# The last four output tiles of a fused attention and gated-MLP kernel: PSUM taken out by ScalarE, a bf16 gate, additions over whole rows

## The chip, the core and the metric

The kernel runs on one core of a Trainium2 chip. The core has five engines with queues of their own: TensorE (PE in the profile; its weight loads are PEld), VectorE (DVE), ScalarE (ACT), GpSimd (POOL) and SyncE (SP), which here only issues DMAs. The metric is the device time of one launch in microseconds, as the median of several runs. The profile comes from one profiled execution with a time of its own.

## The reference

Two blocks read the same normalised input and are multiplied together:

```python
xn = _layernorm(x, axis=-1)                      # x: 1 x 2048 x 640
qkv = xn @ wqkv                                  # 32 heads of 20
p = softmax(q k^T * 20**-0.5)
s = (p v) @ wo                                   # 2048 x 640
h = sigmoid(xn @ w_gate) * (xn @ w_up)           # 2048 x 1728
g = silu(h @ w_down)                             # 2048 x 640
return x + s * g
```

## The kernel before

Attention is worked off in 32 blocks: a block is one group of four heads and one chunk of 512 query rows. TensorE makes scores into PSUM. ScalarE takes most of them through Exp, and VectorE computes the others with integer operations on bf16 bits (L1030, L1033, L1036). TensorE multiplies the results with v into the bank `oacc`. Between these pieces a planner written in Python places the MLP of the four chunks, the projections of the next groups and the output projection of finished rows. It steps through a modelled time, decides what each engine does next from modelled durations, and so writes out the fixed order of the instructions on each engine. Only this order counts on the chip; between engines semaphores hold what depends on what.

**The gate.** `mk_down` (L720) multiplies the hidden layer with `w_down`. ScalarE takes tanh of it, and VectorE makes from tanh and PSUM four times the gate (L737 for the last chunk, L741 for the others). The gate of the first three chunks goes to DRAM and comes back later. That of the last chunk stays in SBUF as fp32, in two buffers of the tag `wgu`, which no longer hold weights by then: `gq_last(t4)` (L714) gives the 640 columns of row tile `t4`.

**The end stage.** The last block needs a path of its own, since nothing is left that could hide its latency. The last chunk has 512 rows, in four tiles of 128 rows (`t4` 0 to 3) with 640 columns. Before the end TensorE has done the output projection of these tiles for all but the last of five slices of the contraction (`early`, L1056), as its time allowed. It lies in PSUM in two parts: columns 0 to 511 of tile `t4` in the bank `mains[t4]`, and columns 512 to 639 of tiles 0, 1 together in `rest[0]`, of tiles 2, 3 in `rest[1]`. The list `chain` (L1135) then orders what is left. Each entry names an engine, a modelled duration, the function and the entries that it comes after. An engine runs its entries in the order of the list:

- `e_on`, `e_tr`, `e_scale`, `e_back`, `e_o`: in two halves of 256 rows the attention's result is taken out of `oacc`, transposed, divided by the sums, transposed back and copied into `oU`; half 0 by VectorE, half 1 by ScalarE where the two are named.
- `e_late(i)`: TensorE adds the last slice for the tiles of half `i`: first the two banks of 512 columns (L1093), then the two pieces of 128 columns (L1100). Of half 1, all narrow matmuls are done here.
- `t_main(t4)` (L1106): VectorE multiplies the bank with 0.25 and the gate into SBUF as bf16 (L1107); for tiles 0 and 1 GpSimd adds the 512 columns to the rows of x (L1110).
- `t_done(i)` (L1128): `t_rest` does the same for the 2 x 128 columns left over (VectorE L1113; the addition L1117 by GpSimd for half 0, by VectorE for half 1). For half 1 `t_last` (L1121) adds the 512 columns on VectorE. `t_out` (L1123) issues the store of each tile of 160 KB: even tiles from SyncE's queue, odd ones from ScalarE's.

The rows of x (`tail`) are loaded into SBUF long before (L1049) and hold the sum in the end. The products lie in `hfl`, the buffer of the hidden layer (`hT` in the profile), which is not needed any more; x and the sum lie in `xnT`.

So VectorE's order in the end stage is: products of banks 0 and 1, narrow product of half 0, products of banks 2 and 3, narrow product of half 1, narrow addition of half 1, additions of tiles 2 and 3. GpSimd's is: additions of tiles 0 and 1 and the narrow addition of half 0.

Of the kernel before, what the change touches and what calls it, by code (L numbers as in the profile page):

```python
# [52 lines left out]
def kernel(  # L53
# [22 lines left out]
    HD = D // 2  # L76
# [3 lines left out]
    def act_imm(o, i, func, scale):  # L80
        zero = mybir.ImmediateValue(dtype=FP32, value=0.0)
        sc = mybir.ImmediateValue(dtype=FP32, value=scale)
        return nc.scalar.add_instruction(mybir.InstActivation(  # L83
            func=func, name=nc.get_next_instruction_name(), engine=ENG.Activation,
            ins=[nc.scalar.lower_ap(i), zero, sc, zero], outs=[nc.scalar.lower_ap(o)]))
# [119 lines left out]
    with tc.tile_pool(name="ln", bufs=2) as lp, \  # L205
# [149 lines left out]
        for c in range(NQC):  # L355
            ks = range(4 * c, 4 * c + 4)
            st = [Step(s_stats, (k,), {"ACT": 1.83} if k in ACT_STATS else {"DVE": 1.03},
                       (table,) if k in ACT_STATS else (), X_AT[k], late=L_ST * c) for k in ks]
# [22 lines left out]
        t = 0.0  # L381
# [37 lines left out]
    def misc_ps():  # L419
        return bank[got_bank[0]]  # L420
# [48 lines left out]
    def mark(*e):  # L469
        return lambda t: ev_at.__setitem__(e, t)  # L470

    def cols(out, lhsT, rhs, start, stop):
        for j in range(0, P, 32):
            nc.tensor.matmul(out[j:j + 32, :], lhsT=lhsT[:, j:j + 32], rhs=rhs, start=start, stop=stop,  # L474
                             tile_position=(0, j), skip_group_check=True)
# [235 lines left out]

    gq_l = []

    def gq_last(t4):  # L714
        if len(gq_l) == t4 // 2:
            w = w2.tile([P, 2, KD, 2 * P], BF16, tag="wgu", bufs=2, name="gql")
            gq_l.append(w.rearrange("p i k f -> p (i k f)").bitcast(FP32))
        return gq_l[t4 // 2][:, t4 % 2 * D:(t4 % 2 + 1) * D]

    def mk_down(c, t4, h, at):  # L720
        st = {}
        tt = 4 * c + t4

        def alloc():
            st["ps"] = misc_ps()

        def mm(kf):
            cols(st["ps"][:, 0:HD], hT[:, kf, t4 * P:(t4 + 1) * P], wd[:, kf, h * HD:(h + 1) * HD],
                 kf == 0, kf == NFT - 1)

        def th():
            st["td"] = w2.tile([P, HD], BF16, tag="td", bufs=2, name="td")
            act_imm(st["td"], st["ps"][:, 0:HD], ACT.Tanh, 0.25)

        def ev():
            if c == NQC - 1:
                return nc.vector.scalar_tensor_tensor(out=gq_last(t4)[:, h * HD:(h + 1) * HD], in0=st["td"], scalar=1.0,  # L737
                                                      in1=st["ps"][:, 0:HD], op0=ALU.add, op1=ALU.mult)
            flush("o")
            gqs = w2.tile([P, HD], FP32, tag="gqs", bufs=3, name="gqs")  # L740
            ins = nc.vector.scalar_tensor_tensor(out=gqs, in0=st["td"], scalar=1.0, in1=st["ps"][:, 0:HD],  # L741
                                                 op0=ALU.add, op1=ALU.mult)
            nc.sync.dma_start(out=gq_dram[tt * P:(tt + 1) * P, h * HD:(h + 1) * HD], in_=gqs)
            return ins
        return Item([("PE", alloc, [(0.14, lambda kf=kf: mm(kf)) for kf in range(NFT)]),
                     ("ACT", 0.32, th), ("DVE", 0.40, ev, "free", mark("d", c, t4, h))], at, pre=[("h", c, kf) for kf in range(NFT)])
# [215 lines left out]
    def flush(*kinds):  # L962
        for x in [x for x in pool_q if x[1] in kinds]:
            pool_q.remove(x)
            x[2]()
# [74 lines left out]
    hfl = hT.rearrange("p k s -> p (k s)")  # L1040
    EX = D - 512
    xl = xfl[:, (NQC - 1) * KD * QC:(NQC - 1) * KD * QC + 4 * D]
    tail = []
# [8 lines left out]
    mains = [bank[0], bank[1], scA[1][:, 0, :], scA[1][:, 1, :]]  # L1052
# [38 lines left out]
    def e_late(i):  # L1091
        for t4 in (2 * i, 2 * i + 1):
            late_mm(mains[t4], t4, slice(0, 512))  # L1093
        if i:
            rest[1] = psum.tile([P, QC], FP32, name="rest1", tag="scA0")
            for kd in range(KD - 1):
                for t4 in (2, 3):
                    early(ex(t4), t4, slice(512, D), kd, t4 == 2)
        for t4 in (2 * i, 2 * i + 1):
            late_mm(ex(t4), t4, slice(512, D))  # L1100

    tmps = [hfl[:, t4 * 512:(t4 + 1) * 512] for t4 in range(4)]
    tmp = hfl[:, 4 * 512:4 * 512 + 4 * EX].rearrange("p (t e) -> p t e", e=EX)
    xg = xl.rearrange("p (t u) -> p t u", u=D)

    def t_main(t4):  # L1106
        nc.vector.scalar_tensor_tensor(out=tmps[t4], in0=mains[t4], scalar=0.25, in1=gq_last(t4)[:, 0:512],  # L1107
                                       op0=ALU.mult, op1=ALU.mult)
        if t4 < 2:
            nc.gpsimd.tensor_tensor(out=tail[t4][:, 0:512], in0=tmps[t4], in1=tail[t4][:, 0:512], op=ALU.add)  # L1110

    def t_rest(i):
        nc.vector.scalar_tensor_tensor(out=tmp[:, 2 * i:2 * i + 2, :],  # L1113
                                       in0=rest[i][:, 0:2 * EX].rearrange("p (t e) -> p t e", e=EX),
                                       scalar=0.25, in1=gq_l[i].rearrange("p (t u) -> p t u", u=D)[:, :, 512:D],
                                       op0=ALU.mult, op1=ALU.mult)
        (nc.vector if i else nc.gpsimd).tensor_tensor(out=xg[:, 2 * i:2 * i + 2, 512:D], in0=tmp[:, 2 * i:2 * i + 2, :],  # L1117
                                                      in1=xg[:, 2 * i:2 * i + 2, 512:D], op=ALU.add)

    def t_last(t4):  # L1120
        nc.vector.tensor_tensor(out=tail[t4][:, 0:512], in0=tmps[t4], in1=tail[t4][:, 0:512], op=ALU.add)  # L1121

    def t_out(t4):  # L1123
        r = slice(4 * (NQC - 1) * P + t4 * P, 4 * (NQC - 1) * P + (t4 + 1) * P)
        eng = nc.sync if t4 % 2 == 0 else nc.scalar
        eng.dma_start(out=out2[r, :], in_=tail[t4])

    def t_done(i):  # L1128
        t_rest(i)
        for t4 in (2 * i, 2 * i + 1):  # L1130
            if i:
                t_last(t4)
            t_out(t4)

    chain = [("DVE", 0.34, lambda: e_on(0), ()), ("ACT", 0.34, lambda: e_on(1), (0,)),  # L1135
# [2 lines left out]
             ("PE", 0.20, lambda: e_back(0), (4,)), ("PE", 0.20, lambda: e_back(1), (5,)),  # L1138
             ("DVE", 0.27, lambda: e_o(0), (6,)), ("ACT", 0.34, lambda: e_o(1), (7,)),
             ("PE", 0.54, lambda: e_late(0), (8,), (0, 1)),  # L1140
             ("DVE", 0.63, lambda: t_main(0), (10,)), ("DVE", 0.63, lambda: t_main(1), (10,)),
             ("DVE", 0.7, lambda: t_done(0), (10,)),
             ("PE", 1.1, lambda: e_late(1), (9,), (0, 1, 2, 3)),
             ("DVE", 0.63, lambda: t_main(2), (14,)), ("DVE", 0.63, lambda: t_main(3), (14,)),
             ("DVE", 1.3, lambda: t_done(1), (14,))]
    chain_end = {}

    def chain_next(eng):
        k = next((k for k, x in enumerate(chain) if x[0] == eng and k not in chain_end), None)
        return k if k is not None and all(chain_end.get(d, 1e9) <= now for d in chain[k][3]) and (  # L1150
            len(chain[k]) < 5 or not any(x[4] in chain[k][4] for x in fill)) else None
# [17 lines left out]
    with tc.manual_schedule(engines={ENG.PE, ENG.Activation, ENG.DVE, ENG.Pool}):  # L1169
# [55 lines left out]
        def run_item(it, eng):  # L1225
            op = it.ops[it.i]
            did = op[2]()
            if eng == "DVE":
                beat(did, len(op) > 3 and op[3] == "free")
            end = now + op[1]  # L1230
            free[eng] = end
            finish(it, end)
            if len(op) > 4:
                op[4](end + EL)
            return op
# [4 lines left out]
        while len(chain_end) < len(chain) or fill or items or glu_items or any(it.i < len(it.ops) for it in active):  # L1240
# [37 lines left out]
            for eng in ("ACT", "DVE"):  # L1278
                if free[eng] > now:
                    continue  # L1280
                k = chain_next(eng) if chain_at <= now else None
# [10 lines left out]
                if it is not None:  # L1292
                    op = run_item(it, eng)
# [50 lines left out]
                elif pass_ok:  # L1344
                    dve_last = "pass"
                    d = dve_pass[0]
                    k = d["k"]
# [24 lines left out]
            if free["PE"] <= now:  # L1372
# [87 lines left out]
                if nxt == "M":  # L1460
# [9 lines left out]
                    op = cur.ops[cur.i]  # L1470
# [68 lines left out]
```

## Time and profile before

| what | value |
|---|---|
| time, median of 3 runs | 802.37 us (801.88 to 803.19) |
| the profiled execution, its own time | 803.29 us |
| its span, from the first to the last instruction | 801.6 us |
| mean granted TensorE clock | 0.999 |
| busy: TensorE, VectorE, ScalarE, GpSimd | 779.8, 770.1, 781.8, 96.4 us |
| the chain that ended last: TensorE, ScalarE, VectorE | 45%, 41%, 7% of the span |
| last block's attention result leaves `oacc` (L1068) | at 790.91 us |
| first and last instruction of VectorE on the end's products and sums | 793.80 and 798.34 us |

Times in the trace count from the first instruction of the program. A row of the timeline or of the groups names the engine, the line of the kernel, the operation, what it writes and reads by the names of the tiles, and the shapes as partitions x elements. A row that ends in x2 holds two instructions in a row of the same form. Line L83 is a helper, `act_imm`, that issues many of ScalarE's instructions. The small q behind an engine (SPq, ACTq) is its sequencer, which waits and issues DMAs.

### The profile page before, as it was taken

To read this page: it belongs to the slowest core of one execution; us is meant where nothing else is said; L and a number is where in the kernel's file an instruction comes from. 1 tells how busy PE (TensorE), PEld (TensorE's weight loads), DVE (VectorE), ACT (ScalarE), POOL (GpSimd) and SP (SyncE) were. 2 spreads that over 40 slices of the span, in tenths; PEclk is the share of its full clock that TensorE was granted. 3 is DMA by queue.
4 is the path that set the end of the run, shared out by engine and by line. 5 is a ranking of instruction groups with operands and counts; after the bars stand their busy time and mean duration, and the time that the engine had idled before them with its cause. 6 is when DMAs were issued, how large, how long until landed. Compare 5 with 4: busy or idle time off the path is not lost.

```text
span 801.6 us, 25384 instructions
## 1 busy us (share of the span) xinstructions
PE 779.8 (97%) x10465; PEld 284.4 (35%) x10465; DVE 770.1 (96%) x1246; ACT 781.8 (98%) x992; POOL 96.4 (12%) x203
## 2 busy tenths in 40 slices
PE   8899999999999999999999999999999999999997
PEld 5523333333433323334332332333333233333332
DVE  7798999999999999989999999999999999999997
ACT  8799999999999999999999999999999999999994
POOL 7200000000000000000000000000000100502302
PEclk9999999999999999999999999999999999999999
DMA  5441212223122223222113232222311332331421
GB/s 162 132 131 49 69 40 73 66 67 81 47 62 67 73 72 100 53 60 65 53 46 89 58 87 73 73 81 62 98 36 61 91 89 53 102 107 23 141 70 55
DMA packets 91851, 60.47 MB, mean 75 GB/s; under 512 B 34891, under 2 KB 85627, under 8 KB 91735
## 3 DMA queue, kind: packets, MB, share of 16 engines
q1 hardware_dynamic: 91447, 58.52, 26.1%
q8 instruction: 82, 1.34, 0.7%
q14 instruction: 34, 0.28, 0.1%
q10 hardware_dynamic: 288, 0.33, 0.1%
HBM read 45.18 MB, written 11.09 MB: 70 GB/s over the span
## 4 chain that ended last, share of the span: by engine, by line
PE 45%; ACT 41%; DVE 7%; issue 5%; DMA 1%; SPq 0%; POOL 0%; DVEq 0%; ACTq 0%; POOLq 0%
ACT pt L83 33%; PE bk L474 18%; PE scA L900 14%; PE oacc L937 9%; ACT px L83 4%; DVE iv L1336 2%; ACT tnh L83 2%; DVE pb L1036 1%; ACT td L83 1%; PE bk L900 1%; DVE pb L1033 1%; PE tp L293 1%; DVE pb L1030 0%; DMA lt<-ld 0%; DMA ld<-on 0%
## 5 line engine op out<-in xcount | busy, mean ns | idle before, releaser
L83 ACT ACTIVATE pt<-scA 128x1024 bf16<-128x1024 f32 (+1 forms) x709 | 708.7, 1188 | 0.7 <-PE bk L900 0.3
L1336 DVE TENSOR_SCALAR iv<-bk 128x512 int16<-128x512 f32 x499 | 332.2, 683 | 12.1 <-PE bk L900 9.6
L900 PE MATMUL scA<-q,kT 32*128 32x512 bf16 x1412 | 275.8, 382 | 8.8 <-ACT pt L83 3.3
L900 PE MATMUL bk<-q,kT 32*128 32x512 bf16 x636 | 207.3, 383 | 0.2 <-DVE iv L1336 0.2
L900 PEld LDWEIGHTS <-kT 32*128 32x128 bf16 x2048 | 88.4, 91 | 262.4 <-issue 251.1
L937 PE MATMUL oacc<-pt,v 128*21 128x512 bf16 x1412 | 178.5, 381 | 0.7 <-ACT pt L83 0.7
L937 PE MATMUL oacc<-pb,v 128*21 128x512 bf16 x998 | 160.8, 382 | 0.0
L474 PE MATMUL bk<-xnT,wgu 128*32 128x512 bf16 x2160 | 157.3, 383 | 0.5 <-DVE iv L1336 0.2
L1036 DVE TENSOR_TENSOR pb<-iv,pb 128x2048 bf16<-128x2048 bf16 (+1 forms) x125 | 151.8, 1214 | 0.7
L990 POOL TENSOR_TENSOR on_bf<-on,rl 128x128 bf16<-128x128 f32 x116 | 54.3, 472 | 626.8 <-DVE iv L1336 189.1
L83 ACT ACTIVATE px<-bk 128x512 bf16<-128x512 f32 x137 | 102.1, 762 | 1.7 <-POOL hT L1178 1.6
L474 PE MATMUL bk<-wd,hT 128*32 128x320 bf16 x1792 | 87.0, 302 | 0.1
L1030 DVE TENSOR_SCALAR pb<-iv 128x2048 int16<-128x2048 int16 (+1 forms) x125 | 86.0, 688 | 0.4
L1033 DVE TENSOR_SCALAR pb<-iv 128x2048 int16<-128x2048 int16 (+1 forms) x125 | 85.9, 688 | 0.0
L937 PEld LDWEIGHTS <-v 128*21 128x21 bf16 x2547 | 53.6, 91 | 76.2 <-issue 53.6
L474 PEld LDWEIGHTS <-wgu 128*32 128x32 bf16 x2160 | 44.5, 95 | 64.3 <-issue 46.3
L474 PEld LDWEIGHTS <-hT 128*32 128x32 bf16 x1792 | 37.5, 95 | 38.2 <-issue 32.7
L474 PE MATMUL bk<-xnT,wu 128*32 128x512 bf16 x640 | 48.5, 383 | 0.6 <-DVE iv L1336 0.2
L937 PE MATMUL oacc<-px,v 128*21 128x512 bf16 x137 | 47.0, 381 | 0.0
L83 ACT ACTIVATE tnh<-bk 128x512 bf16<-128x512 f32 (+1 forms) x56 | 43.4, 776 | 0.1
L691 DVE SCALAR_TENSOR_TENSOR hT<-tnh,bk 128x512 bf16<-128x512 bf16 x52 | 35.4, 680 | 1.0 <-PE bk L900 0.3
L655 PE MATMUL bk<-wv,xnT 128*128 128x160 bf16 x280 | 29.4, 235 | 0.6 <-ACT px L83 0.6
(120 smaller groups left out, 406.2 us busy)
## 6 DMA issues: line engine op xcount, KB each, us to landing
rl<-rd SPq DMA_DIRECT2D x124, 64.0 KB
wgu<-in_B_w_gate_dram SPq DMA_DIRECT2D x24, 320.0 KB
wgu<-in_B_w_up_dram SPq DMA_DIRECT2D x24, 320.0 KB
gq_dram<-gqs SPq DMA_DIRECT2D x24, 160.0 KB
xnT<-gq_dram SPq DMA_DIRECT2D x12, 320.0 KB
xt<-in_A_x_dram SPq DMA_DIRECT2D x16, 160.0 KB
xnT<-in_A_x_dram SPq DMA_DIRECT2D x16, 160.0 KB
out_dram<-xnT SPq DMA_DIRECT2D x14, 160.0 KB
```

The source lines that it names most:

```text
L83: return nc.scalar.add_instruction(mybir.InstActivation(func=func, name=nc.get_next_instruction_name(), engine=ENG.Activation, ins=[nc.sca ...
L293: nc.tensor.transpose(out=tps[k][:, kd, :], in_=xns[k][:, kd * P:(kd + 1) * P], identity=ident)
L474: nc.tensor.matmul(out[j:j + 32, :], lhsT=lhsT[:, j:j + 32], rhs=rhs, start=start, stop=stop, tile_position=(0, j), skip_group_check=True)
L655: nc.tensor.matmul(st["ps"][:, i * 2 * GC:(i + 1) * 2 * GC], lhsT=xn_tok(tts[i], kd), rhs=wvs[pr][:, kd, :], start=(kd == 0), stop=(kd == ...
L691: return nc.vector.scalar_tensor_tensor(out=hT[0:fs, kf, :], in0=st["t"][0:fs, :], scalar=1.0, in1=st["u"][0:fs, :], op0=ALU.add, op1=ALU. ...
L900: nc.tensor.matmul(dst, lhsT=kTs[gc_of(b)[0] % 2][32 * j:32 * j + 32, kt * P:(kt + 1) * P], rhs=qts[b % 3][32 * j:32 * j + 32, :], start=T ...
L937: nc.tensor.matmul(oacc[32 * j:32 * j + DH + 1, :], lhsT=lhsT, rhs=u["src"], start=first, stop=last, tile_position=(0, 32 * j), skip_group ...
L990: ins = nc.gpsimd.tensor_tensor(out=on_bf[:, cs], in0=on[:, cs], in1=rl[:, cs], op=ALU.mult)
L1030: ins = nc.vector.tensor_scalar(out=pb[:, 0, :, :].bitcast(I16), in0=iv, scalar1=0x7F80, scalar2=1, op0=ALU.bitwise_and, op1=ALU.bitwise_or)
L1033: ins = nc.vector.tensor_scalar(out=pb[:, 1, :, :].bitcast(I16), in0=iv, scalar1=0x007F, scalar2=0x3F00, op0=ALU.bitwise_and, op1=ALU.bitw ...
L1036: ins = nc.vector.tensor_tensor(out=pb[:, 1, :, :], in0=iv.bitcast(BF16), in1=pb[:, 1, :, :], op=ALU.mult)
L1336: beat(nc.vector.tensor_scalar(out=d["iv"][:, j, :], in0=bank[bk], scalar1=B_OFF, scalar2=0.0, op0=ALU.add, op1=ALU.max))
```

## The change

All of it concerns the last chunk.

- The gate of the last chunk is kept as bf16 in one buffer, tile after tile, in place of fp32 in two.
- The products get one layout, 640 columns for each tile, in place of four pieces of 512 and one of 4 x 128.
- Of each half, the odd tile's bank (`mains[1]`, `mains[3]`) is first copied out of PSUM by ScalarE as bf16, times 0.25 (`t_copy`). VectorE then multiplies the copy with the gate in SBUF. The even tile's bank is multiplied straight out of PSUM, as before.
- The narrow addition of half 0 goes from GpSimd to VectorE. GpSimd keeps the two additions of 512 columns.
- Half 1: the narrow addition of 2 x 128 columns and the two of 512 become two additions of 640.
- The stores of tiles 0, 1 and 2 are issued by SyncE, that of tile 3 by ScalarE.

```diff
-    def gq_last(t4):
-        if len(gq_l) == t4 // 2:
+    def gq_last():
+        if not gq_l:
             w = w2.tile([P, 2, KD, 2 * P], BF16, tag="wgu", bufs=2, name="gql")
-            gq_l.append(w.rearrange("p i k f -> p (i k f)").bitcast(FP32))
-        return gq_l[t4 // 2][:, t4 % 2 * D:(t4 % 2 + 1) * D]
+            gq_l.append(w.rearrange("p i k f -> p (i k f)")[:, 0:4 * D].rearrange("p (t u) -> p t u", u=D))
+        return gq_l[0]
...
-                return nc.vector.scalar_tensor_tensor(out=gq_last(t4)[:, h * HD:(h + 1) * HD], in0=st["td"], scalar=1.0,
+                return nc.vector.scalar_tensor_tensor(out=gq_last()[:, t4, h * HD:(h + 1) * HD], in0=st["td"], scalar=1.0,
...
-    tmps = [hfl[:, t4 * 512:(t4 + 1) * 512] for t4 in range(4)]
-    tmp = hfl[:, 4 * 512:4 * 512 + 4 * EX].rearrange("p (t e) -> p t e", e=EX)
+    tmp = hfl[:, 0:4 * D].rearrange("p (t u) -> p t u", u=D)
     xg = xl.rearrange("p (t u) -> p t u", u=D)
 
+    def t_add(eng, t4, a, b):
+        eng.tensor_tensor(out=tail[t4][:, a:b], in0=tmp[:, t4, a:b], in1=tail[t4][:, a:b], op=ALU.add)
+
+    def t_copy(t4):
+        act_imm(tmp[:, t4, 0:512], mains[t4], ACT.Copy, 0.25)
+
     def t_main(t4):
-        nc.vector.scalar_tensor_tensor(out=tmps[t4], in0=mains[t4], scalar=0.25, in1=gq_last(t4)[:, 0:512],
+        if t4 % 2:
+            nc.vector.tensor_tensor(out=tmp[:, t4, 0:512], in0=tmp[:, t4, 0:512], in1=gq_last()[:, t4, 0:512], op=ALU.mult)
+        else:
+            nc.vector.scalar_tensor_tensor(out=tmp[:, t4, 0:512], in0=mains[t4], scalar=0.25, in1=gq_last()[:, t4, 0:512],
+                                           op0=ALU.mult, op1=ALU.mult)
+        if t4 < 2:
+            t_add(nc.gpsimd, t4, 0, 512)
+
+    def t_rest(i):
+        nc.vector.scalar_tensor_tensor(out=tmp[:, 2 * i:2 * i + 2, 512:D],
+                                       in0=rest[i][:, 0:2 * EX].rearrange("p (t e) -> p t e", e=EX),
+                                       scalar=0.25, in1=gq_last()[:, 2 * i:2 * i + 2, 512:D],
                                        op0=ALU.mult, op1=ALU.mult)
...
-        (nc.vector if i else nc.gpsimd).tensor_tensor(out=xg[:, 2 * i:2 * i + 2, 512:D], in0=tmp[:, 2 * i:2 * i + 2, :],
-                                                      in1=xg[:, 2 * i:2 * i + 2, 512:D], op=ALU.add)
-
-    def t_last(t4):
-        nc.vector.tensor_tensor(out=tail[t4][:, 0:512], in0=tmps[t4], in1=tail[t4][:, 0:512], op=ALU.add)
+        if not i:
+            nc.vector.tensor_tensor(out=xg[:, 0:2, 512:D], in0=tmp[:, 0:2, 512:D], in1=xg[:, 0:2, 512:D], op=ALU.add)
...
-        eng = nc.sync if t4 % 2 == 0 else nc.scalar
+        eng = nc.sync if t4 < 3 else nc.scalar
...
             if i:
-                t_last(t4)
+                t_add(nc.vector, t4, 0, D)
             t_out(t4)
...
-             ("DVE", 0.63, lambda: t_main(0), (10,)), ("DVE", 0.63, lambda: t_main(1), (10,)),
-             ("DVE", 0.7, lambda: t_done(0), (10,)),
+             ("ACT", 0.55, lambda: t_copy(1), (10,)),
+             ("DVE", 0.63, lambda: t_main(0), (10,)), ("DVE", 0.35, lambda: t_main(1), (11,)),
+             ("DVE", 0.70, lambda: t_done(0), (10,)),
              ("PE", 1.1, lambda: e_late(1), (9,), (0, 1, 2, 3)),
-             ("DVE", 0.63, lambda: t_main(2), (14,)), ("DVE", 0.63, lambda: t_main(3), (14,)),
-             ("DVE", 1.3, lambda: t_done(1), (14,))]
+             ("ACT", 0.55, lambda: t_copy(3), (15,)),
+             ("DVE", 0.63, lambda: t_main(2), (15,)), ("DVE", 0.35, lambda: t_main(3), (16,)),
+             ("DVE", 1.25, lambda: t_done(1), (15,))]
```

More of the change, by code (lines that the diff above doesn't have):

```diff
@@ L1106, in t_main @@
     def t_main(t4):
-        nc.vector.scalar_tensor_tensor(out=tmps[t4], in0=mains[t4], scalar=0.25, in1=gq_last(t4)[:, 0:512],
-                                       op0=ALU.mult, op1=ALU.mult)
[L1109 to L1117, printed above, removed]
-                                                      in1=xg[:, 2 * i:2 * i + 2, 512:D], op=ALU.add)
```

## The prediction

> **What bounds the kernel now.** I read the page first, for the span and the share of each engine.
>
> ```profile
> span 801.6 us, 25384 instructions
> PE 779.8 (97%) x10465; PEld 284.4 (35%) x10465; DVE 770.1 (96%) x1246; ACT 781.8 (98%) x992; POOL 96.4 (12%) x203
> ```
>
> Three engines are full for nearly the whole span, but the change touches only what comes after the last attention block. The exception is the gate of the last chunk, written earlier by eight instructions. So the second view is the timeline of the end stage. Its columns are start, time, engine, line, operation, out<-in, shapes, count.
>
> ```profile
> 793.37 0.37 ACT L1085 COPY oU<-tp 80x256 bf16<-80x256 bf16 x1 [1.59 <-PE tp L1082]
> 793.38 0.71 PE L1061 MATMUL bk<-wo,oU 128*128 128x512 bf16 x4
> 793.80 1.29 DVE L1107 SCALAR_TENSOR_TENSOR hT<-bk,gql 128x512 bf16<-128x512 f32 x2 [0.55 <-PE bk L1061]
> 794.64 2.26 POOL L1110 TENSOR_TENSOR xnT<-hT,xnT 128x512 bf16<-128x512 bf16 x2 [11.52 <-DVE hT L1107]
> 795.01 0.41 DVE L1113 SCALAR_TENSOR_TENSOR hT<-bk,gql 128x256 bf16<-128x256 f32 x1
> 795.42 1.29 DVE L1107 SCALAR_TENSOR_TENSOR hT<-scA,gql 128x512 bf16<-128x512 f32 x2
> 796.63 0.41 DVE L1113 SCALAR_TENSOR_TENSOR hT<-rest,gql 128x256 bf16<-128x256 f32 x1
> 796.86 0.66 POOL L1117 TENSOR_TENSOR xnT<-hT,xnT 128x256 bf16<-128x256 bf16 x1
> 797.08 0.59 DVE L1117 TENSOR_TENSOR xnT<-hT,xnT 128x256 bf16<-128x256 bf16 x1
> 797.55 0.82 SPq L1126 DMA_DIRECT2D out_dram<-xnT  x2
> 797.55 1.16 ACTq L1126 DMA_DIRECT2D out_dram<-xnT  x2
> 797.59 0.75 DVE L1121 TENSOR_TENSOR xnT<-hT,xnT 128x512 bf16<-128x512 bf16 x2
> ```
>
> VectorE works without a gap from 793.80 to 798.34. The first half's two stores leave at 797.55, when GpSimd's third addition is done (797.52), so all four stores go within 0.8 us (797.55, 797.55, 798.03, 798.37). The third view, the table by windows, shows what that does (the column before the last is the DMA engines' busy share):
>
> ```profile
> 798.25:798.50 0.25, 0.00 (x0) 0.00 (x0) 0.09 (x1) 0.00 (x0) 0.00 (x0) 1.00 0.39 148
> 799.75:800.00 0.25, 0.00 (x0) 0.00 (x0) 0.00 (x0) 0.00 (x0) 0.00 (x0) 0.50 1.06 394
> 800.00:800.25 0.25, 0.00 (x0) 0.00 (x0) 0.00 (x0) 0.00 (x0) 0.00 (x0) 0.50 0.42 144
> ```
>
> The DMA engines are full from 798.35 to 800.2, and the span ends 1.4 us after the last packet, at 801.6. So the end has two limits close together: VectorE's last addition, and 640 KB of stores that start late. A lone store of the same 160 KB (issued 779.88) had its packets from 0.86 to 1.42 us after its issue. By that the last store, issued 798.37, would have been through at 799.79 without the others ahead of it. The backlog costs 0.4 us.
>
> The fourth view is the timeline where GpSimd and VectorE meet.
>
> ```profile
> 780.77 1.22 DVE L1036 TENSOR_TENSOR pb<-iv,pb 128x2048 bf16<-128x2048 bf16 x1
> 781.27 1.85 POOL L995 TENSOR_TENSOR on_bf<-on,rl 128x512 bf16<-128x512 f32 x1 [18.24 <-DMA rl<-rd]
> 781.90 1.40 DVE L814 TENSOR_TENSOR xnT<-otmp,xnT 128x320 bf16<-128x320 bf16 x1
> ...
> 629.38 0.47 POOL L990 TENSOR_TENSOR on_bf<-on,rl 128x128 bf16<-128x128 f32 x1
> 629.48 0.91 DVE L1030 TENSOR_SCALAR pb<-iv 128x2048 int16<-128x2048 int16 x1
> 629.79 0.92 POOL L990 TENSOR_TENSOR on_bf<-on,rl 128x128 bf16<-128x128 f32 x1
> ```
>
> The addition L814 takes 0.31 us alone and here 1.40: it ends 0.18 us after the GpSimd instruction that came first (783.12). At 629 they take turns in the order of their starts: GpSimd, then VectorE (0.91 instead of 0.68), then GpSimd (0.92 instead of 0.46). In the end stage L1117 on VectorE took 0.59 beside GpSimd; by the two L1121 (0.41 for 512 columns, 0.335 apart) it takes 0.28 alone. VectorE instructions that read PSUM are not held: L1107 keeps 0.68 to 0.69 beside L1110. So an instruction of VectorE on SBUF alone waits until GpSimd's running one is through, and the other way round.
>
> The Trainium skill has this rule too (SBUF — State Buffer, "Who interferes with whom"): a VectorE instruction with two SBUF inputs and a GpSimd instruction that reads SBUF exclude each other, and the first to issue keeps the port pair for its whole length. The trace agrees on the exclusion, but not quite on the length: L1117 on VectorE ends 0.15 after GpSimd's recorded end, less than its own 0.28, so the pair comes free some 0.13 before that end. Taken by the letter, each wait below would be 0.13 longer, and the forecast would be 802.7.
>
> **The change part by part.**
>
> Gate as bf16: eight L737 of 0.48 us now write bf16. L796 writes bf16 in the same shape in 0.48, so 0, between -0.01 and +0.01 for each. One tile instead of two takes a wait away, if any.
>
> ScalarE copies of pieces 1 and 3: ScalarE is idle after 793.74. A 128x512 ACTIVATE from PSUM took 0.575 on an idle ScalarE (L174 at 17.70); the Exp of that shape takes 0.59 at the least, 0.77 at the median of a busy stage. I take 0.575 to 0.59, since ScalarE is idle here; 0.77 stays as the upper end. Piece 0's matmul starts at 793.384 and VectorE 0.417 later. Piece 1's starts at 793.600, so the copy runs from 794.02 to 794.60. VectorE follows ScalarE by 0.033 (L741 at 571.98), so the multiply of piece 1 is ready at 794.62 to 794.64. VectorE has been free since 794.49, and behind that multiply stand, in order, everything else of VectorE and thereby three stores. Copy 3 (from about 795.4 to 796.0) is hidden; its multiply comes after 796.7.
>
> Multiplies 1 and 3 from SBUF: 0.41 (bf16 L1121) instead of 0.69, adding 0.33 between ends instead of 0.60. That saves 0.27 each on VectorE's path.
>
> First half's narrow addition, POOL to VectorE: off GpSimd 0.66, onto VectorE 0.03 + 0.28 = 0.31 ahead of piece 2. Second half: L1117 (0.59, alone 0.28) and two L1121 become two additions of 640 columns: 0.48 and then 0.40 between ends, by the slope of the L1121 (0.27 of streaming for 512).
>
> Store of piece 1 moves from ScalarE's queue to SyncE's: SyncE issues at 0.40 to 0.48 spacing (0.33 long), and its three are more than that apart below. ScalarE has no other work then.
>
> The sum if nothing is held: multiply 0 ends 794.49, multiply 1 795.05, rest 795.38, narrow addition 795.70, multiply 2 796.30, multiply 3 796.63, rest 796.97, additions 797.48 and 797.88. That is 0.46 earlier than 798.34, and with stores no longer in a bunch, packets through at 797.91 + 1.42 = 799.33: 0.85 us saved.
>
> But GpSimd now works beside SBUF-only instructions of VectorE. Its first addition starts 0.145 after multiply 0, at 794.64, as before: the same moment at which multiply 1 gets ready. Which comes first is too close to call from durations. In the trace VectorE goes first when it starts 0.05 before GpSimd, GpSimd when it leads by 0.10; the edge lies between -0.05 and +0.10, and here VectorE's start lies between 0.02 before GpSimd's and level with it. That is nearer to VectorE going first.
>
> Forecast, VectorE first: multiply 1 ends 795.05, GpSimd's addition 0 is held and ends 795.05 + 1.15 - 0.14 = 796.06 (0.14 by the held L990). Rest ends 795.38; the narrow addition is ready at 795.42, is held, and ends 796.06 + 0.15 = 796.21 (+0.51). GpSimd's addition 1 follows and ends 796.21 + 1.01 = 797.22. Multiply 2 ends 796.81. Multiply 3 is held until GpSimd is through: 797.22 + 0.28 = 797.50 (+0.36). Rest 797.84, additions 798.35 and 798.75. Stores leave at 796.25, 797.26, 798.39 and 798.78; nothing queues before the last, which is through at 798.78 + 1.42 = 800.20, where the last packet is now (0.05 more if the third is in its way). So the 0.41 that VectorE loses and the 0.4 of the vanished backlog cancel: 0 to +0.1 us. Against the profiled execution (803.29, of which 1.7 lie outside the span) this is 803.3; that execution is 0.92 above the median of the runs, 802.37, so the forecast is **802.5** for the median.
>
> **Rivals.**
>
> GpSimd first. This is the slower side: GpSimd's addition 0 has the port from 794.64 to 795.79, multiply 1 ends 795.79 + 0.28 = 796.07 (+1.02), and GpSimd's addition 1, waiting for it, runs 796.17 to 797.32. The narrow addition, ready at 796.44, ends 797.47; then multiply 2 798.07, multiply 3 798.40, rest 798.74, additions 799.25 and 799.65. Last store 799.68, packets through 801.10: +0.9, 803.3. It decides if the copy takes over about 0.60, or if GpSimd waits for one semaphore less and starts earlier. For it speaks the Exp row's 0.59 and 0.77; against it the 0.575.
>
> No holding: 0.85 saved, 801.5. The three held instructions above speak against it; only if GpSimd's additions held the port for much less than their rows last could it come so.
>
> A dependency kept on whole ranges: the first rest product and the narrow addition write strided columns around piece 1's, and might wait for GpSimd's addition 1. On the rival's order this adds about 0.6: +1.5, 803.9. Against it: L296 on ScalarE (22.20 to 22.90) and on VectorE (21.85 to 22.34) write interleaved columns of one tile at once.
>
> **How the numbers follow.** Chances: VectorE first 0.47, GpSimd first 0.35, no holding 0.06, whole ranges 0.04, something that these views do not show 0.08 (half each way). A difference under 0.2% (1.6 us) is about what a measurement of this kernel can't tell from none. All four cases lie inside it. Outside come 1 in 8 of the GpSimd-first cases by the scatter of the runs (801.88 to 803.19), half of the whole-range ones and the unseen ones: slower 0.04 + 0.02 + 0.05, taken as 0.12; faster 0.01 + 0.04, taken as 0.06; within 0.82. The range 801.4 to 803.9 reaches from the unheld case to GpSimd first with 0.6 of scatter; the likeliest case's own is 802.0 to 803.0.
>
> **What would show it.** Right: the multiply of piece 1 starts within 0.05 of GpSimd's first addition at 794.64; the narrow addition or a multiply on VectorE is over 0.6 long instead of 0.28 or 0.41; the last store leaves near 798.8 and the DMA share stays below full between the stores. Multiply 1 at over 1 us long is the rival. Wrong outright: VectorE's SBUF-only instructions keep their lone lengths beside GpSimd, the ScalarE copy comes later than 794.1, or the span changes before 793.

## The result

The changed kernel takes 803.94 us (median of 15 runs, 803.35 to 804.60), the kernel before 802.59 us beside it (15 runs, 801.88 to 803.58). The ratio is 1.0016, with a 95% interval from 1.0009 to 1.0023: slower by 0.7 to 1.8 us. The interval leaves out 1, so the slowdown is clear of the scatter, and its upper end lies just above the 0.2% under which the prediction looked for the difference. The forecast was 802.5 for a median of 802.37, in a range from 801.4 to 803.9, so an increase of 0.1 where 1.35 came. As written, that range ends 0.04 below 803.94; moved to the median of 802.59 measured beside the change, it is 801.6 to 804.1 and holds it near its upper end. Its rival "GpSimd first" had 803.3, an increase of 0.9.

The profile of the changed kernel has a span of 802.7 us. This is the timeline of its end stage, with the columns as before. The lines of the code have moved: L1115 is the product out of PSUM, L1113 the multiply from SBUF, L1121 the narrow product, L1126 the narrow addition of half 0, L1106 every addition by `t_add`, L1131 the stores, L83 on ScalarE the copies.

```profile
793.88 0.69 DVE L1115 SCALAR_TENSOR_TENSOR hT<-bk,gql 128x512 bf16<-128x512 f32 x1 [0.55 <-PE bk L1061]
794.10 0.60 ACT L83 ACTIVATE hT<-bk 128x512 bf16<-128x512 f32 x1 [0.28 <-PE bk L1061]
794.72 1.15 POOL L1106 TENSOR_TENSOR xnT<-hT,xnT 128x512 bf16<-128x512 bf16 x1 [11.51 <-ACT hT L83]
794.73 1.42 DVE L1113 TENSOR_TENSOR hT<-hT,gql 128x512 bf16<-128x512 bf16 x1 [0.15 <-ACT hT L83]
795.50 0.60 ACT L83 ACTIVATE hT<-scA 128x512 bf16<-128x512 f32 x1 [0.81 <-PE scA L1061]
796.07 0.41 DVE L1121 SCALAR_TENSOR_TENSOR hT<-bk,gql 128x256 bf16<-128x256 f32 x1
796.30 1.15 POOL L1106 TENSOR_TENSOR xnT<-hT,xnT 128x512 bf16<-128x512 bf16 x1 [0.43 <-DVE hT L1113]
796.52 1.07 DVE L1126 TENSOR_TENSOR xnT<-hT,xnT 128x256 bf16<-128x256 bf16 x1
797.52 0.68 DVE L1115 SCALAR_TENSOR_TENSOR hT<-scA,gql 128x512 bf16<-128x512 f32 x1
797.66 2.09 SPq L1131 DMA_DIRECT2D out_dram<-xnT  x3
798.12 0.41 DVE L1113 TENSOR_TENSOR hT<-hT,gql 128x512 bf16<-128x512 bf16 x1
798.45 0.41 DVE L1121 SCALAR_TENSOR_TENSOR hT<-rest,gql 128x256 bf16<-128x256 f32 x1
798.89 0.90 DVE L1106 TENSOR_TENSOR xnT<-hT,xnT 128x640 bf16<-128x640 bf16 x2
799.82 0.38 ACTq L1131 DMA_DIRECT2D out_dram<-xnT  x1
```

Two rows carry it. The multiply of piece 1 (L1113) gets ready at 794.73, 0.01 us after GpSimd's first addition has started, and takes 1.42 us; the same instruction takes 0.41 at 798.12, when GpSimd is idle. The narrow addition (L1126) takes 1.07 beside GpSimd's second addition. The releaser that the view names for GpSimd's first addition, ScalarE's copy, is a coincidence: in every run below that has this addition it starts 0.84 us after the start of VectorE's first product, also where the copy ends 0.1 us sooner.

From here on, times count from the start of VectorE's first product in the same profile, written P0 (793.80 before, 793.88 with the change). In the nanoseconds of the trace VectorE's last addition ended at P0+4.54 before and ends at P0+5.91 now; the span ended at P0+7.77 and ends at P0+8.77. So the end stage is 1.0 us longer, which lies in the interval of the measured difference. That the remaining 0.35 us of the medians is the change's doing is not shown.

The table by windows of the changed kernel (DMA busy share in the column before the last) shows the gain that came with the loss:

```profile
799.25:799.50 0.25, 0.00 (x0) 0.00 (x0) 0.25 (x2) 0.00 (x0) 0.00 (x0) 0.50 0.81 292
799.75:800.00 0.25, 0.00 (x0) 0.00 (x0) 0.04 (x1) 0.00 (x0) 0.00 (x0) 0.50 0.00 0
800.25:800.50 0.25, 0.00 (x0) 0.00 (x0) 0.00 (x0) 0.00 (x0) 0.00 (x0) 0.50 0.93 348
801.00:801.25 0.25, 0.00 (x0) 0.00 (x0) 0.00 (x0) 0.00 (x0) 0.00 (x0) 0.50 0.79 282
```

The stores of the first half are through by 799.5, the DMA engines stand idle, and then the last two pass. From the last addition to the end of the span it is now 2.86 us, where it was 3.23: the backlog of 0.4 us has gone, as the prediction had it.

### The profile page after: what moved, and what is told of

Its sections match the earlier page's. It is cut to its first block, busy times and chain, and to the rows that moved or that the text cites. A ratio compares the mean times of both kernels' runs of the same rounds, so it can differ in the third digit from the quotient of the medians.

```text
span 802.7 us, 25379 instructions
## 1 busy us (share of the span) xinstructions
PE 779.5 (97%) x10460; PEld 284.3 (35%) x10465; DVE 771.4 (96%) x1246; ACT 783.1 (98%) x994; POOL 95.8 (12%) x202
## 3 DMA queue, kind: packets, MB, share of 16 engines
q8 instruction: 82, 1.34, 0.7%
## 4 chain that ended last, share of the span: by engine, by line
PE 44%; ACT 41%; DVE 7%; issue 6%; DMA 1%; POOL 1%; DVEq 0%; ACTq 0%; POOLq 0%; SPq 0%
ACT pt L83 33%; PE bk L474 18%; PE scA L900 13%; PE oacc L937 9%; ACT px L83 5%; DVE iv L1343 2%; ACT tnh L83 2%; DVE pb L1036 1%; ACT td L83 1%; PE bk L900 1%; DVE pb L1033 1%; PE tp L293 1%; DVE pb L1030 0%; DMA lt<-ld 0%; DMA ld<-on 0%
## 5 line engine op out<-in xcount | busy, mean ns | idle before, releaser
L83 ACT ACTIVATE pt<-scA 128x1024 bf16<-128x1024 f32 (+1 forms) x709 | 707.8, 1184 | 0.9 <-PE bk L900 0.5
L1036 DVE TENSOR_TENSOR pb<-iv,pb 128x2048 bf16<-128x2048 bf16 (+1 forms) x125 | 151.7, 1213 | 0.7
L83 ACT ACTIVATE px<-bk 128x512 bf16<-128x512 f32 x137 | 101.6, 758 | 1.7 <-POOL hT L1185 1.6
L83 ACT ACTIVATE tnh<-bk 128x512 bf16<-128x512 f32 (+1 forms) x56 | 43.2, 772 | 0.1
```

The costliest lines, as they stand in the source:

```text
L83: return nc.scalar.add_instruction(mybir.InstActivation(func=func, name=nc.get_next_instruction_name(), engine=ENG.Activation, ins=[nc.sca ...
L1036: ins = nc.vector.tensor_tensor(out=pb[:, 1, :, :], in0=iv.bitcast(BF16), in1=pb[:, 1, :, :], op=ALU.mult)
```

## The experiments

The theory is that of the prediction's rival: a VectorE instruction on SBUF alone and a GpSimd addition exclude each other, who is ready first goes first, and here GpSimd is first by 0.01 us. All lengths below are from one profile each, and every edit moves the line numbers by a few; where a ratio is given, it is against the kernel before on the same chip.

**GpSimd's additions left out**

```diff
-        if t4 < 2:
-            t_add(nc.gpsimd, t4, 0, 512)
```

> The changed kernel without GpSimd's two additions: x is not added to columns 0 to 511 of tiles 0 and 1, all else stays. Times count from the start of VectorE's first product (P0); before, VectorE's last addition ended at P0+4.54 and the span at P0+7.77, with the change at P0+5.91 and P0+8.77. Theory (VectorE's instructions on SBUF alone are held by GpSimd's running addition): the multiply of piece 1 takes 0.41 instead of 1.42, the narrow addition 0.28 instead of 1.07, the last addition ends at P0+4.1, the last store leaves at P0+4.1 and the span ends at P0+6.9. Rival (the multiply is slow by itself, since it reads what ScalarE has just written or the bf16 gate): it still takes 1.42 and the last addition ends at P0+5.1 or later.

```profile
793.75 0.43 DVE L1113 TENSOR_TENSOR hT<-hT,gql 128x512 bf16<-128x512 bf16 x1 [0.15 <-ACT hT L83]
794.54 0.29 DVE L1124 TENSOR_TENSOR xnT<-hT,xnT 128x256 bf16<-128x256 bf16 x1
795.15 0.69 DVE L1115 SCALAR_TENSOR_TENSOR hT<-scA,gql 128x512 bf16<-128x512 f32 x1 [0.32 <-ACT hT L83]
```

In this timeline the multiply takes 0.43 and the narrow addition 0.29, so it is GpSimd that held them, and the rival falls. But the last addition ends at P0+4.54 and the span at P0+7.40, 0.4 us later than the theory's sum. The third row says why: the product of bank 2 waited 0.32 us for ScalarE's copy of bank 3, which the sum had taken as hidden.

**VectorE ready 0.10 us sooner**

```diff
-        act_imm(tmp[:, t4, 0:512], mains[t4], ACT.Copy, 0.25)
+        n = 384 if t4 == 1 else 512
+        act_imm(tmp[:, t4, 0:n], mains[t4][:, 0:n], ACT.Copy, 0.25)
```

> ScalarE copies only 384 of the 512 columns of piece 1 (the last 128 columns of that product are then made from what lay in the buffer), so that VectorE's multiply of piece 1 is ready about 0.10 us earlier, ahead of GpSimd's first addition by about 0.1 instead of behind it by 0.01. Times from the start of VectorE's first product (P0). Theory (who starts first has the port, the other waits, and they take turns): the multiply takes 0.41, GpSimd's first addition about 1.33 instead of 1.15; now the narrow addition is held (about 0.8) and the multiply of piece 3 (about 0.75); the last addition ends at P0+4.85 and the span at P0+7.7, as before the change. Rival (GpSimd comes first whatever the order, as soon as it is ready): the multiply still ends near P0+2.2, and the last addition at P0+5.8 to 5.9.

```profile
794.73 0.42 DVE L1114 TENSOR_TENSOR hT<-hT,gql 128x512 bf16<-128x512 bf16 x1
794.83 2.49 POOL L1106 TENSOR_TENSOR xnT<-hT,xnT 128x512 bf16<-128x512 bf16 x2 [11.25 <-ACT hT L83]
795.53 0.79 DVE L1127 TENSOR_TENSOR xnT<-hT,xnT 128x256 bf16<-128x256 bf16 x1
796.86 0.75 DVE L1114 TENSOR_TENSOR hT<-hT,gql 128x512 bf16<-128x512 bf16 x1
```

Here the order is turned round, and this is the course that the prediction took for the likeliest: multiply 0.42, narrow addition 0.79, multiply of piece 3 0.75. GpSimd's first addition takes 1.34 and its second 1.20. The last addition ends at P0+4.87, the span at P0+7.75, as expected to 0.05 us and level with the kernel before.

**Where the edge lies**

The same with `n = 480`, which makes VectorE ready 0.016 us ahead of GpSimd's start instead of 0.010 behind it.

> ScalarE copies 480 of the 512 columns of piece 1 (32 columns of that product are made from what lay in the buffer), so that the multiply is ready about 0.017 before GpSimd's recorded start instead of 0.010 behind it. Where is the edge? If the recorded starts decide: the multiply takes 0.42, GpSimd's first addition about 1.42, the last addition ends at P0+4.9 to 4.95 and the span at P0+7.8. If GpSimd has the port some 0.02 or more before its recorded start: the multiply takes 1.44, the last addition ends at P0+5.9.

```profile
793.50 0.57 ACT L83 ACTIVATE hT<-bk 128x480 bf16<-128x480 f32 x1 [0.28 <-PE bk L1061]
794.11 0.43 DVE L1114 TENSOR_TENSOR hT<-hT,gql 128x512 bf16<-128x512 bf16 x1
794.12 2.58 POOL L1106 TENSOR_TENSOR xnT<-hT,xnT 128x512 bf16<-128x512 bf16 x2 [11.52 <-ACT hT L83]
794.90 0.80 DVE L1127 TENSOR_TENSOR xnT<-hT,xnT 128x256 bf16<-128x256 bf16 x1
```

As finely as these runs can tell, the earlier recorded start goes first: VectorE here, 0.016 us ahead, GpSimd with the change, 0.010 ahead, and in the next run 0.007 ahead. A copy shorter by 0.026 us turns the order, and the span ends at P0+7.84 instead of 8.77.

**GpSimd's additions in pieces of 256 columns**

```diff
-            t_add(nc.gpsimd, t4, 0, 512)
+            for a in (0, 256):
+                t_add(nc.gpsimd, t4, a, a + 256)
```

> GpSimd's two additions of 512 columns are each made as two of 256 (0.66 each by the row L1117 of before). Times from the start of VectorE's first product (P0). Theory (the port is held for one instruction, and the two engines take turns): the multiply of piece 1 waits for one piece only and takes about 0.93 instead of 1.42; GpSimd's second piece is held in its turn (about 0.9 to 1.0); the narrow addition takes about 0.3, the multiply of piece 3 about 0.9; the last addition ends at P0+5.1 and the span at P0+8.0. Rival (GpSimd keeps the port while it has work queued): the multiply of piece 1 takes 1.4 to 1.6, as with the change, and the last addition ends at P0+5.9 or later.

```profile
793.86 2.77 POOL L1106 TENSOR_TENSOR xnT<-hT,xnT 128x256 bf16<-128x256 bf16 x4 [11.51 <-ACT hT L83]
793.87 0.94 DVE L1113 TENSOR_TENSOR hT<-hT,gql 128x512 bf16<-128x512 bf16 x1 [0.15 <-ACT hT L83]
796.01 0.91 DVE L1113 TENSOR_TENSOR hT<-hT,gql 128x512 bf16<-128x512 bf16 x1
```

The multiply waits for one piece of GpSimd's and not for its queue: 0.94, expected 0.93. The four pieces take 0.67, 0.85, 0.71 and 0.66; the second waited for the multiply and the third, a little, for the narrow addition. Last addition at P0+5.15, span end at P0+8.02. So the two engines take turns by instruction, and a shorter instruction on the one shortens the wait of the other.

**All additions on VectorE**

```diff
-        if t4 < 2:
-            t_add(nc.gpsimd, t4, 0, 512)
...
-        if not i:
-            nc.vector.tensor_tensor(out=xg[:, 0:2, 512:D], in0=tmp[:, 0:2, 512:D], in1=xg[:, 0:2, 512:D], op=ALU.add)
...
-            if i:
-                t_add(nc.vector, t4, 0, D)
+            t_add(nc.vector, t4, 0, D)
```

> All four tiles are added by VectorE over 640 columns; GpSimd does nothing in the end stage. Otherwise as with the change. Times from the start of VectorE's first product (P0). Theory: nothing is held, the multiply of piece 1 takes 0.41, the two additions of half 0 take 0.49 each (0.40 apart) where a narrow addition of 1.07 stood; the last addition ends at P0+4.7 and the span at P0+7.6, 0.2 less than before the change and 1.2 less than with it; ratio to before 0.9997, with 1 inside the interval. Rival (the loss lies elsewhere, in the copies or the whole-row additions): the last addition ends later than P0+5.5 and the ratio stays at 1.001 or more.

The end stage came out as the theory had it: last addition at P0+4.73, span end at P0+7.60, 0.17 less than before and 1.17 less than with the change. The ratio is 1.0008 (0.9999 to 1.0017), which shows no gain over the kernel before; a gain of 0.17 us is far below what it can show. The rival falls by the end stage, where its last addition would have come later than P0+5.5.

**The gate alone**

In the kernel before, only the gate becomes bf16, in one buffer:

```diff
-        if len(gq_l) == t4 // 2:
+        if not gq_l:
             w = w2.tile([P, 2, KD, 2 * P], BF16, tag="wgu", bufs=2, name="gql")
-            gq_l.append(w.rearrange("p i k f -> p (i k f)").bitcast(FP32))
-        return gq_l[t4 // 2][:, t4 % 2 * D:(t4 % 2 + 1) * D]
+            gq_l.append(w.rearrange("p i k f -> p (i k f)"))
+        return gq_l[0][:, t4 * D:(t4 + 1) * D]
...
-                                       scalar=0.25, in1=gq_l[i].rearrange("p (t u) -> p t u", u=D)[:, :, 512:D],
+                                       scalar=0.25, in1=gq_l[0][:, 2 * i * D:(2 * i + 2) * D].rearrange("p (t u) -> p t u", u=D)[:, :, 512:D],
```

> The kernel before with one part of the change alone: the last chunk's gate as bf16 in one buffer. Times from the start of VectorE's first product (P0). Theory (the gate's type costs nothing where the other operand comes from PSUM): the eight products that write the gate stay at 0.48, the products of 512 columns at 0.68 to 0.69, the last addition ends at P0+4.54, the span at P0+7.77. Rival (a bf16 gate makes these products faster, or brings a wait): the products of 512 columns change by over 0.05, or the last addition moves by over 0.1.

The eight products that write the gate stay at 0.48 (median), the products out of PSUM at 0.68 to 0.69, the last addition at P0+4.54, the span end at P0+7.79 (before 7.77). Where the other operand comes from PSUM, the gate's type costs and brings nothing. What it is worth to the multiply from SBUF no run shows, since none made that multiply with a gate in fp32.

**The narrow addition alone on VectorE**

```diff
-        (nc.vector if i else nc.gpsimd).tensor_tensor(out=xg[:, 2 * i:2 * i + 2, 512:D], in0=tmp[:, 2 * i:2 * i + 2, :],
-                                                      in1=xg[:, 2 * i:2 * i + 2, 512:D], op=ALU.add)
+        nc.vector.tensor_tensor(out=xg[:, 2 * i:2 * i + 2, 512:D], in0=tmp[:, 2 * i:2 * i + 2, :],
+                                in1=xg[:, 2 * i:2 * i + 2, 512:D], op=ALU.add)
```

> The kernel before with one part of the change alone: the narrow addition of half 0 on VectorE in place of GpSimd. Times from the start of VectorE's first product (P0). Theory (held by turns): the narrow addition is ready at P0+1.65, waits for GpSimd's first addition and ends at P0+2.14 (0.49 long, alone 0.28); GpSimd's second addition waits for it in turn and ends near P0+3.15; then nothing is held, L1117 of half 1 takes 0.28 instead of 0.59, the last addition ends at P0+4.66 (before: 4.54), but the stores no longer leave in a bunch and the span ends at P0+7.53, 0.24 less than before. Rival (the loss of VectorE's time decides): the span ends later than before by about 0.1, at P0+7.9.

```profile
794.58 2.31 POOL L1110 TENSOR_TENSOR xnT<-hT,xnT 128x512 bf16<-128x512 bf16 x2 [11.27 <-DVE hT L1107]
795.39 0.48 DVE L1117 TENSOR_TENSOR xnT<-hT,xnT 128x256 bf16<-128x256 bf16 x1
797.44 0.29 DVE L1117 TENSOR_TENSOR xnT<-hT,xnT 128x256 bf16<-128x256 bf16 x1
```

Held for 0.2 us (0.48), then free (0.29 instead of 0.59): last addition at P0+4.66, span end at P0+7.57. That is 0.12 later on VectorE and 0.2 earlier at the end, since the stores no longer leave together. The theory holds, and the rival, that VectorE's time decides, falls. The ratio, 0.9999 (0.9989 to 1.0008), can't show 0.2 us.

**The product of bank 2 ahead of the copy of bank 3**

This starts from the run without GpSimd's additions. The numbers in brackets set only the planner's order; the entry 16 added to the copy's keeps it behind the product in the list and makes no wait on the chip by itself.

```diff
-             ("ACT", 0.55, lambda: t_copy(3), (15,)),
-             ("DVE", 0.63, lambda: t_main(2), (15,)), ("DVE", 0.35, lambda: t_main(3), (16,)),
+             ("DVE", 0.63, lambda: t_main(2), (15,)),
+             ("ACT", 0.55, lambda: t_copy(3), (15, 16)), ("DVE", 0.35, lambda: t_main(3), (17,)),
```

> As the run without GpSimd's additions (x is not added to columns 0 to 511 of tiles 0 and 1), but the product of bank 2 stands ahead of ScalarE's copy of bank 3 in the list. In that run the product of bank 2 waited until P0+2.25, when the copy was done. Times from the start of VectorE's first product (P0). Theory (the wait comes from the order of the list: the product waits on ScalarE's semaphore in place of TensorE's): it starts at P0+1.85, the last addition ends at P0+4.13 and the span at P0+7.0. Rival (VectorE and ScalarE cannot read the two banks of one PSUM tile at once, or the bank is not ready): it still starts near P0+2.25 and the last addition ends near P0+4.54, unless the copy now waits for the product.

```profile
794.85 0.68 DVE L1115 SCALAR_TENSOR_TENSOR hT<-scA,gql 128x512 bf16<-128x512 f32 x1
795.57 0.60 ACT L83 ACTIVATE hT<-scA 128x512 bf16<-128x512 f32 x1 [1.75 <-DVE hT L1115]
```

The product starts at P0+1.85, but now the copy waits for it, until P0+2.57, and the last addition comes at P0+4.89 instead of P0+4.54. So the theory's half on the order was right and its time wrong: whichever of the two reads stands first in the list, the other waits on its semaphore. The two banks are halves of one PSUM tile (`scA[1]`); `bank[0]` and `bank[1]`, which are tiles of their own, were read at once at 794.10 in the changed kernel, where the product and the copy also write the same buffer `hT`, so writing that buffer is not the cause. The Trainium skill (PSUM — Partial Sum Buffer, "PSUM bank collisions raise a hardware error") reports that two engines on different banks run clean. By that the chip would not ask for this wait, only the program does; no run here took it away.

**A version meant to beat both**

All additions on VectorE, banks 1, 2 and 3 copied by ScalarE, and VectorE's order changed so that the narrow product fills the gap ahead of the multiply of piece 1. Against the all-VectorE version:

```diff
-        if t4 % 2:
+        if t4:
...
-        t_rest(i)
...
-             ("DVE", 0.63, lambda: t_main(0), (10,)), ("DVE", 0.35, lambda: t_main(1), (11,)),
-             ("DVE", 0.70, lambda: t_done(0), (10,)),
+             ("DVE", 0.63, lambda: t_main(0), (10,)), ("DVE", 0.35, lambda: t_rest(0), (10,)),
+             ("DVE", 0.35, lambda: t_main(1), (11,)), ("DVE", 0.85, lambda: t_done(0), (10,)),
...
-             ("ACT", 0.55, lambda: t_copy(3), (15,)),
-             ("DVE", 0.63, lambda: t_main(2), (15,)), ("DVE", 0.35, lambda: t_main(3), (16,)),
-             ("DVE", 1.25, lambda: t_done(1), (15,))]
+             ("ACT", 0.55, lambda: t_copy(2), (16,)), ("ACT", 0.55, lambda: t_copy(3), (16,)),
+             ("DVE", 0.35, lambda: t_main(2), (17,)), ("DVE", 0.35, lambda: t_rest(1), (16,)),
+             ("DVE", 0.35, lambda: t_main(3), (18,)), ("DVE", 0.90, lambda: t_done(1), (16,))]
```

> A version meant to beat both: VectorE adds all four tiles over 640 columns, GpSimd does nothing; ScalarE also copies bank 2, so that in half 1 both large products are made from SBUF; VectorE's order is product 0, rest of half 0, product 1, additions 0 and 1, product 2, rest of half 1, product 3, additions 2 and 3. Times from the start of VectorE's first product (P0). Theory: no gap ahead of product 1 and no holding; the last addition ends at P0+3.96 if the copy of bank 2 starts at P0+1.42, when that bank is ready, and at P0+4.15 if it starts at P0+1.62 as the copy of bank 3 did; the span ends 2.83 after the last store, at P0+6.8 to 7.0, 0.8 to 0.95 less than before; ratio 0.9988 to 0.9990. Rival (something else sets the end: the stores' transfers or the waits on ScalarE): the span ends at P0+7.4 or later and the ratio is 0.9995 or more.

> The reordered version once more, beside the change itself, since its first comparison (0.9999, 0.9990 to 1.0008) is as wide as the gain its end stage showed (span end at P0+7.0 against 7.77 before). Theory (the end stage sets the gain, the rest is scatter of what lies before it): P0+7.0 again, ratio to before 0.9990, the interval mostly below 1. Rival (the version also makes what comes before P0 later, by as much as it gains): P0 in the profile lies over 0.5 later than in the others and the ratio stays at 1.000.

> The change itself once more on the same chip. Theory (held by GpSimd's first addition; its end stage is 1.0 us longer than before): the multiply of piece 1 again takes 1.42, the last addition ends at P0+5.91, the span at P0+8.77, ratio 1.0012. Rival (who comes first is a toss-up from run to run): the multiply takes 0.42 this time, the last addition ends near P0+4.95 and the ratio is near 1.000.

The timeline of the second run of this version:

```profile
793.80 0.69 DVE L1115 SCALAR_TENSOR_TENSOR hT<-bk,gql 128x512 bf16<-128x512 f32 x1 [0.55 <-PE bk L1061]
794.41 0.41 DVE L1119 SCALAR_TENSOR_TENSOR hT<-bk,gql 128x256 bf16<-128x256 f32 x1
794.74 0.42 DVE L1113 TENSOR_TENSOR hT<-hT,gql 128x512 bf16<-128x512 bf16 x1
795.42 1.08 ACT L83 ACTIVATE hT<-scA 128x512 bf16<-128x512 f32 x2 [0.81 <-PE scA L1061]
797.06 0.89 DVE L1106 TENSOR_TENSOR xnT<-hT,xnT 128x640 bf16<-128x640 bf16 x2
797.98 0.37 ACTq L1127 DMA_DIRECT2D out_dram<-xnT  x1
```

Both profiles have the last addition at P0+4.15 and the span end at P0+7.0, 0.77 us less than before the change, by the second of the two values expected: the copy of bank 2 started at P0+1.62. The ratios to the kernel before are 0.9999 (0.9990 to 1.0008) and 0.9993 (0.9984 to 1.0002), above the expected 0.9988 to 0.9990, and both intervals hold 1. So that it is faster than the kernel before is shown for the end stage of two profiles and not for the time. Faster than the change it is: in the second comparison, on one chip, the medians are 802.60 and 804.24 us.

The change itself, once more:

```profile
794.59 1.15 POOL L1106 TENSOR_TENSOR xnT<-hT,xnT 128x512 bf16<-128x512 bf16 x1 [11.52 <-ACT hT L83]
794.60 1.43 DVE L1113 TENSOR_TENSOR hT<-hT,gql 128x512 bf16<-128x512 bf16 x1 [0.15 <-ACT hT L83]
```

It again took 1.43 for the multiply, ended its last addition at P0+5.91 and the span at P0+8.77, with a ratio of 1.0016 (1.0007 to 1.0024). GpSimd was first by 0.009 us. In these two profiles of the change and in the run with pieces of 256 the order came out the same, so nothing speaks for a toss-up from run to run.

Much of the width of these intervals comes from before the end stage. P0 lay at 795.42 in the first profile of this version and at 793.80 in the second, with the same program; over all profiles it lies between 792.90 and 795.42. In the first one VectorE ran within 0.1 us of the kernel before at 753.7 us and was 1.7 behind at 763.5. Between the two, VectorE waited twice for TensorE (0.31 us at 757.2 and 0.65 at 761.3), where the kernel before shows no such wait. Then its multiply L1036 took 1.69 instead of 1.22 beside an operation of GpSimd (L995) that had started ahead of it at 761.23; in the kernel before the multiply was the one ahead. So the order of the two engines, which decides the end stage, can add to the scatter as well. Why TensorE came later was not followed up.

All end stages, in us after P0:

| kernel | last addition | last store issued | span end |
|---|---|---|---|
| before | 4.54 | 4.57 | 7.77 |
| the change, both times | 5.91 | 5.94 | 8.77 |
| GpSimd's additions left out | 4.54 | 4.57 | 7.40 |
| copy of 384 columns | 4.87 | 4.91 | 7.75 |
| copy of 480 columns | 4.96 | 4.99 | 7.84 |
| GpSimd in pieces of 256 | 5.15 | 5.19 | 8.02 |
| all additions on VectorE | 4.73 | 4.76 | 7.60 |
| gate alone | 4.54 | 4.57 | 7.79 |
| narrow addition alone | 4.66 | 4.69 | 7.57 |
| product 2 ahead of copy 3 | 4.89 | 4.92 | 7.75 |
| reordered, both times | 4.15 | 4.18 | 7.00, 7.01 |

## Why the prediction was right and wrong

Right that the ratio stays under 0.2%, to which it gave most of the chance, but that speaks little for the mechanism, since all four of its cases lay inside. Its remark that a measurement can hardly tell so little from none did not hold here: the interval leaves out 1. Wrong in the course that it took for the likeliest, and so in the time: 0.1 us forecast, 1.35 measured. By the prediction's own sign, a multiply 1 at over 1 us long, it was the rival that came.

- **The step that failed** is the one that it called too close to call: who comes first at 794.64. It put the multiply's readiness at 794.62 to 794.64, so 0.82 to 0.84 after P0, with a copy of 0.575 to 0.59. The copy took 0.598 and the multiply was ready at P0+0.846. GpSimd started at P0+0.836, as forecast (0.84). The prediction named the copy's length of "about 0.60" as the point from which its rival decides, and the copy came to that.

**Where the copy's length went wrong.** The row L174 at 17.70, taken for a copy on an idle ScalarE, starts while the row ahead of it still runs (17.61 + 0.19 = 17.80).

```profile
17.61 0.19 ACT L271 ACTIVATION_READ_ACCUMULATOR sq<-xt,nm 128x1 f32 x1
17.70 0.57 ACT L174 ACTIVATE aq<-psq 128x512 bf16<-128x512 f32 x1
30.98 0.60 ACT L83 ACTIVATE px<-bk 128x512 bf16<-128x512 f32 x1 [1.64 <-POOL hT L1178]
```

The trace before has two Exps of that shape that do start on an idle ScalarE, at 30.98 and at 706.06, and both took 0.597. With that, the prediction's own sum gives 794.02 + 0.597 + 0.033 = 794.65, behind GpSimd's 794.64. Why the L174 row is shorter no run shows.

- The prediction also leaned on the middle of a wide bracket for the edge, 0.05 ahead to 0.10 behind. The runs put it between 0.016 ahead and 0.007 behind, which holds equal recorded starts, and the lean towards VectorE had no ground.
- **The rest of both courses held.** The forecast course, measured with the copy of 384 or 480 columns, ends its last addition at P0+4.87 and 4.96 (forecast 4.95) and the span at P0+7.75 and 7.84 (forecast 7.77 to 7.87). The rival's sum gave P0+5.85 and +0.9 us; the profile shows P0+5.91 and +1.0.
- **The stores.** That a backlog of 0.4 us would vanish was right, and shown apart from the rest by the narrow addition alone: VectorE 0.12 later, the end 0.2 earlier.
- **The gate** at 0 was right.
- **"Copy 3 is hidden" was wrong**, though it did no harm to the forecast. The product of bank 2 waits for it, until P0+2.25, in the run without GpSimd's additions. In the forecast course VectorE is busy about as long (until P0+2.32 with the copy of 384 columns), in the change longer. The case without holding was therefore overrated: 0.4 us saved and not 0.85.
- The dependency on whole ranges did not show: the narrow product of half 0 started right behind the multiply, at 796.07, while GpSimd's addition 1 was still to come.
- **The rule of the Trainium skill** (SBUF — State Buffer, "Who interferes with whom") that the first to issue keeps the port pair, and that issue order decides who blocks, is borne out by an order that 0.026 us turned. The section writes the first of these for certain fast modes of VectorE ("2-port perf mode") and says of `tensor_tensor` that it contends; that it holds for the `TENSOR_TENSOR` here is what the rows show. Its length was better taken from the rows: with the copy of 384 columns the narrow addition ended 0.15 after GpSimd's recorded end and the multiply of piece 3 0.28, less than their lone 0.29 and 0.42.

## What to carry to other kernels

Before an operation is changed from a PSUM operand to SBUF operands to make it faster, look at what GpSimd runs at that moment: out of PSUM it ran beside GpSimd at 0.69 us, out of SBUF it took 0.41 alone and up to 1.42 beside a GpSimd addition of 1.15. When two such instructions get ready within some hundredths of a microsecond, work out both orders and give neither the benefit of the doubt. Better, change the program so that the order doesn't matter, with the additions on one engine (span end at P0+7.60 against 8.77); shorter pieces on GpSimd only made the loss smaller (8.02). A duration is best taken from a row in the same situation, here on an engine that was idle before; the end of the row ahead shows whether it was. And compare end stages from a common instruction in the trace, since a stage that gains 0.8 us can vanish in the scatter of the 790 us ahead of it.

## What was not expected of the hardware

- The order between VectorE and GpSimd was settled by recorded starts 0.007 to 0.016 us apart, came out the same in two profiles of the change taken at different times, and is worth 0.93 us (P0+8.77 against P0+7.84).
- Two engines reading different banks of one PSUM tile were run one after the other by the program's semaphores, whichever came first, at a cost of 0.32 us in the run without GpSimd's additions (VectorE waiting); with the order turned the last addition came 0.35 later still. No run shows that the chip asks for this wait.
- A ScalarE copy of 128x512 out of PSUM takes 0.60 us, of 480 columns 0.57 and of 384 columns 0.49: 0.83 ns for each column and about 0.17 us fixed.
